# A second MLP product with five of its seven block products in matmuls of 512 columns and six rotating accumulator banks

## The chip, the cores and the metric

The kernel runs on one core of a Trainium2 chip. The metric is the device time of one execution in microseconds. A core has a matrix engine (PE, TensorE, whose weight loads are listed as PEld), a vector engine (DVE, VectorE), a scalar engine (ACT, ScalarE), GpSimd (POOL), and queues for DMA, here mostly SP's. Matmuls accumulate in PSUM, which has eight banks of 512 float32 columns on 128 partitions.

## The reference

```python
def _B_ref(x, w1, b1, w2, b2):
    h = _layernorm(x, axis=-1)                  # (B, S, D), S = 2048, D = 512
    u = jnp.einsum("bsd,sf->bdf", h, w1) + b1   # F = 1792
    u = _gelu(u)
    y = jnp.einsum("bdf,fs->bds", u, w2) + b2
    return y.transpose(0, 2, 1)

h = x + _A_ref(_layernorm(x), ...)   # linear attention with 32 heads and a learned feature map
out = h + _B_ref(_layernorm(h), w1, b1, w2, b2)
```

What changes is the product with `w2` ("the second product"): out of 1792 by 512 values of `u` and 1792 by 2048 weights it makes 2048 by 512 sums, to which `b2` and `h` are added.

## The kernel before

The attention block comes first, then the first MLP product (with `w1`, lines 62 to 64, matmuls of 512 columns), then GELU, then the second product, which is the last stage.

All products are of float32 accuracy on a faster matmul type: each operand is split into a high part, rounded to that type, and a low part, the rest. A product is the sum of high x high, high x low and low x high, so three matmuls.

The second product cuts the 2048 output rows into 16 tiles of 128 rows and takes them in 8 pairs (`sp`). The 1792 rows of `w2` are 14 tiles, taken in 7 pairs (`p`), so that there are 56 steps (`STEPS`), pair by pair. A step multiplies a 2 by 2 block matrix of weights (blocks of 128 x 128) with a 2 by 2 block matrix of `u` (blocks of 128 x 256, `HD` = 256 being half of the 512 columns). Instead of eight block products it makes seven, by the Strassen-Winograd scheme: seven weight operands (four of them sums of blocks) and seven operands of `u` (prepared once, `UB`), and a few additions at the end of each pair.

Weights are streamed in groups of two steps (`GRP` = 2, `stream_w2`): two loads of 256 KB on SP's queue into `wraw` (three buffers), four sums on DVE (lines 777 to 780, for both steps at once, 256 elements each), then the high part `whi` on ACT (line 57, 1792 elements) and the low part `wlo` on DVE (line 58). `whi` and `wlo` have two buffers each, so a group's buffers are filled again once PE has read the group two before.

Each product of a step is three matmuls of 256 columns (`product`, line 789) into one half of one of four banks; partial sums that belong to the same output accumulate in the same half, over all 7 steps of the pair. The pairs use two sets of four banks in turn (`ps_b`, or `ps_f` and `ps_q`). In a pair's last step the products are taken by bank, and then a copy on ACT (line 820) and five DVE operations (821 to 825) combine the banks, with `b2` added, into `ot`, and two DMAs on POOL's queue add `ot` to `out`, where `h` was stored before. The last pair instead adds to copies of its two output tiles (`hb`, lines 830 to 847), takes its last two steps together by bank, and stores the result.

The order of instructions on each engine in this stage is not the program's: the framework plans it when the kernel is built, in order of the times it expects, so PE may take a product's matmuls later than the loops name them.

Of the kernel before, what the change touches and what calls it, by code (L numbers as in the profile page):

```python
# [9 lines left out]
F32 = mybir.dt.float32  # L10
F32R = mybir.dt.float32r
AF = mybir.ActivationFunctionType
ALU = mybir.AluOpType
# [4 lines left out]
P = 128  # L18
S, D, H, DH, F = 2048, 512, 32, 16, 1792
NT = S // P  # L20
KD = D // P
NF = F // P
NG = 8
NPR = 2 * NG
Q_AT = (4, 6, 8, 9, 11, 13)
# [8 lines left out]
def block_kernel(ctx: ExitStack, tc: tile.TileContext, x, xT, wT, phic, wo, w1, b1, w2, b2,  # L34
                 kvmask, ident_in, out):
    nc = tc.nc
# [7 lines left out]
    mhalf = cst.tile([P, 4], F32, name="mhalf")  # L44
    b1s = cst.tile([P, NF], F32, name="b1s")
    b2s = cst.tile([P, NT], F32, name="b2s")
# [21 lines left out]
    ps_q = ctx.enter_context(tc.tile_pool(name="ps_q", bufs=2, space=PSUM, side="right"))  # L68
# [19 lines left out]
    wvl = wp.tile([P, KD, D], F32R, name="wvl")  # L88
    zacc = wp.tile([P, NG, P], F32, name="zacc")
    ps_k = a1.enter_context(tc.tile_pool(name="ps_k", bufs=2, space=PSUM))  # L90
# [85 lines left out]
    def k_ops(t, o):  # L176
        PK[t] = kk.tile([P, NG, P], F32, name="pk", bufs=len(V_NOT) + 3)
        run(logit_ops(o, PK[t], False))
# [180 lines left out]
    q = {"mm": 0, "logits": 0, "exp": 0, "sum": 0}  # L359
# [6 lines left out]
    def q_logits(lag):  # L366
        n = q["logits"]
        if n < min(NT, q["mm"] - lag + NT * (q["mm"] == NT)):
            EQ[n] = big.tile([P, NG, P], F32, name="eq", tag="big")
            q["logits"] += 1  # L370
# [28 lines left out]
    for t in range(3, NT - 1):  # L399
        if t + 2 < NT:  # L400
            raw = load_x(t + 2)
# [38 lines left out]
    def s_ez(t):  # L440
        EZ[t] = az.tile([P, NG, P], F32, name="ez")
        nc.gpsimd.tensor_mul(EZ[t], EQ[t], zB)  # L442
# [69 lines left out]
    ps_f = ctx.enter_context(tc.tile_pool(name="ps_f", bufs=2, space=PSUM, reuse_waits="tile"))  # L512
# [79 lines left out]
        split(HN[t][:, 0], HN[t][:, 1], hn, nc.gpsimd)  # L592

    w1v = w1.rearrange("(k p) f -> p k f", p=P)
    w2v = w2.rearrange("(k p) s -> p k s", p=P)

    LATER = []

# [15 lines left out]
    PU, WI, LO = {}, {}, []  # L614
    FN, FL = [0] * (NF // 2), [0] * (NF // 2)

# [90 lines left out]

    NP = NF // 2  # L710
    HD = D // 2
    up = ctx.enter_context(tc.tile_pool(name="up", bufs=1, side="right", reuse_waits="tile"))
    uo = ctx.enter_context(tc.tile_pool(name="uo", bufs=2, side="right", reuse_waits="tile"))
    ws = ctx.enter_context(tc.tile_pool(name="ws", bufs=2, side="right", reuse_waits="tile"))
    ur = ctx.enter_context(tc.tile_pool(name="ur", bufs=4, side="right", reuse_waits="tile"))
    ut = ctx.enter_context(tc.tile_pool(name="ut", bufs=1, side="right", reuse_waits="tile"))
    ps_b = ctx.enter_context(tc.tile_pool(name="ps_b", bufs=4, space=PSUM, reuse_waits="tile"))
# [3 lines left out]
    U, UB, far = {}, {}, {}  # L721
# [39 lines left out]
    hp = ctx.enter_context(tc.tile_pool(name="hp", bufs=1, reuse_waits="tile"))  # L761

    STEPS = [(sp, p) for sp in range(NT // 2) for p in range(NP)]
    GRP = 2
    AW = {}

    def stream_w2(n):
        steps = STEPS[n:n + GRP]
        raw = ws.tile([P, GRP, 7, P], F32, name="wraw", bufs=3)
        wh_ = ws.tile([P, GRP, 7, P], F32R, name="whi")  # L770
        wl_ = ws.tile([P, GRP, 7, P], F32R, name="wlo")
        for i, (sp, p) in enumerate(steps):
            nc.sync.dma_start(raw[:, i, 0:4].rearrange("p (k i) s -> p k (i s)", k=2),
                              w2v[:, 2 * p:2 * p + 2, sp * 2 * P:(sp + 1) * 2 * P])
            AW[sp, p] = wh_[:, i], wl_[:, i]
        with tc.issue_after(LO[-18]):
            nc.vector.tensor_add(raw[:, :, 4], raw[:, :, 0], raw[:, :, 2])
            nc.vector.tensor_sub(raw[:, :, 0], raw[:, :, 1], raw[:, :, 0])
            nc.vector.tensor_sub(raw[:, :, 5], raw[:, :, 4], raw[:, :, 1])
            nc.vector.tensor_sub(raw[:, :, 6], raw[:, :, 3], raw[:, :, 5])  # L780
        split(wh_, wl_, raw, nc.vector)


    PROD = ((1, 1, 0, 0, True), (2, 6, 2, 1, True), (3, 3, 3, 1, True), (4, 4, 2, 0, False), (0, 0, 1, 0, True),
            (5, 5, 0, 1, False), (6, 2, 3, 0, False))

    def product(o, a, b, start, stop):
        for i, (x, y) in enumerate(((0, 0), (0, 1), (1, 0))):
            nc.tensor.matmul(o, a[x], b[:, y], start=start and i == 0, stop=stop and i == 2, skip_group_check=True)  # L789

    def products(sp, ps, order):
        for a, b, bk, half, opens in order:
            for p in ps:
                wh_, wl_ = AW[sp, p]
                product(bank[bk][:, half], (wh_[:, a], wl_[:, a]), UB[p, b], p == 0 and opens, p == NP - 1)

    def flat(a):
        return a.rearrange("p k d -> p (k d)")

    for n, (sp, p) in enumerate(STEPS):  # L800
        t = 2 * sp
        last = t + 2 == NT
        if n % GRP == 0:
            stream_w2(n)
        if p == 0:
            pools = [ps_f, ps_f, ps_q, ps_q] if sp % 2 else [ps_b] * 4
            bank = [pool.tile([P, 2, HD], F32, name="py", tag="pu") for pool in pools]
        if p < NP - 1 - last:
            products(sp, [p], PROD)
            continue  # L810
        if p < NP - 1:
            continue
        by_bank = sorted(PROD, key=lambda m: m[2:4])
        e = uo.tile([P, 2, HD], F32, name="e")
        u2 = uo.tile([P, HD], F32, name="u2", bufs=1)
        u3 = uo.tile([P, HD], F32, name="u3")
        if not last:
            products(sp, [p], by_bank)
            ot = uo.tile([P, 2, 2, HD], F32, name="ot", bufs=1)
            nc.scalar.activation(e[:, 1], bank[0][:, 0], AF.Copy)  # L820
            nc.vector.tensor_add(u2, bank[0][:, 1], e[:, 1])
            nc.vector.tensor_add(u3, bank[1][:, 0], u2)
            nc.vector.tensor_add(e[:, 0], bank[2][:, 0], u2)
            for i, add in enumerate((u3.unsqueeze(1).to_broadcast([P, 2, HD]), e)):
                nc.vector.scalar_tensor_tensor(ot[:, i], bank[2 + i], b2s[:, t + i:t + i + 1], add,  # L825
                                               op0=ALU.add, op1=ALU.add)
                nc.gpsimd.dma_start(out[(t + i) * P:(t + i + 1) * P, :], flat(ot[:, i]), accum_op=ALU.add)  # L827
            continue

        hb = [hp.tile([P, 2, HD], F32, name=f"hb{i}") for i in range(2)]  # L830
        for i in range(2):
            nc.sync.dma_start(flat(hb[i]), out[(t + i) * P:(t + i + 1) * P, :])
            nc.vector.tensor_scalar(hb[i], hb[i], b2s[:, t + i:t + i + 1], None, op0=ALU.add)
        products(sp, [p - 1, p], by_bank)
        nc.scalar.activation(e[:, 1], bank[0][:, 0], AF.Copy)
        nc.vector.tensor_add(hb[1][:, 1], bank[0][:, 0], hb[1][:, 1])
        nc.vector.tensor_add(u2, bank[0][:, 1], e[:, 1])
        nc.vector.tensor_add(hb[1][:, 0], u2, hb[1][:, 0])
        nc.vector.tensor_add(u3, bank[1][:, 0], u2)
        nc.vector.tensor_add(hb[0], hb[0], u3.unsqueeze(1).to_broadcast([P, 2, HD]))  # L840
        nc.vector.tensor_add(hb[0][:, 0], bank[2][:, 0], hb[0][:, 0])
        nc.vector.tensor_add(hb[1][:, 0], bank[2][:, 0], hb[1][:, 0])
        nc.vector.tensor_add(hb[0][:, 1], bank[2][:, 1], hb[0][:, 1])
        nc.sync.dma_start(out[t * P:(t + 1) * P, :], flat(hb[0]))
        for k, q in ((0, nc.scalar), (1, nc.sync)):
            nc.vector.tensor_add(hb[1][:, k], bank[3][:, k], hb[1][:, k])
            q.dma_start(out[(t + 1) * P:NT * P, k * HD:(k + 1) * HD], hb[1][:, k])


def _layout(A_x, A_wqkv, A_w_phi, A_wo, B_w1, B_b1, B_w2, B_b2):  # L850
    x = np.asarray(A_x)[0]
    wqkv = np.asarray(A_wqkv)
    phi = np.asarray(A_w_phi)

    phic = np.concatenate([phi.reshape(4, P, DH).transpose(1, 0, 2).reshape(P, 64),
                           np.kron(np.eye(8), np.ones((DH, 1)))], axis=1).astype(np.float32)
    mask = np.zeros((P, 64), np.float32)
    for a in range(P // DH):
        for c in range(2):
            f = (2 * c + a % 2) * DH  # L860
            mask[a * DH:(a + 1) * DH, f:f + DH] = 1.0

    wo = np.asarray(A_wo).reshape(2, 4, 2, 32, D).transpose(2, 0, 1, 3, 4).reshape(D, D)
    return {
        "x": x,
        "xT": x.reshape(NT, P, KD, P).transpose(0, 3, 2, 1),
        "wT": wqkv.T,
        "phic": phic,
        "wo": wo,
        "w1": np.asarray(B_w1),  # L870
        "b1": np.asarray(B_b1).reshape(NF, P).T,
        "w2": np.asarray(B_w2),
        "b2": np.asarray(B_b2).reshape(NT, P).T,
        "kvmask": mask,
        "ident": np.eye(P, dtype=np.float32),
    }
# [18 lines left out]
```

## Time and profile before

| | |
|---|---|
| time, median of 3 runs | 534.46 us (534.25 to 535.26) |
| span of the profiled execution, first to last instruction | 532.6 us |
| its own whole time | not recorded apart from the span; the median run is 1.8 us above the span |
| mean granted TensorE clock | 0.998 |
| second product's matmuls | from 385.8 us to the last start at 526.8 us |
| matmuls in all | 3616 |

Times in the profile are in microseconds from the span's start. A row of the timeline has start, duration, engine, line, operation, output and inputs, shapes and the count of instructions merged into it; in brackets stands the time for which the engine was idle before it and what ended that. Matmuls are pipelined, so consecutive ones overlap in the records, and their cost is the distance from start to start. The rows that matter are in the prediction.

### The profile page before, as it was taken

How to read it: one execution, taken by the hardware profiler on the slowest of the kernel's cores; microseconds unless marked ns; L12 is line 12 of the kernel's file. 1: busy time of each engine (PE TensorE's matmuls, PEld its weight loads, DVE VectorE, ACT ScalarE, POOL GpSimd, SP SyncE). 2: the span in 40 equal slices, each digit the busy share in tenths (PEclk: the TensorE clock that was granted, in tenths of full speed). 3: DMA queues.
4: the chain of work that ended last, by engine and by line, in shares of the span. 5: the costliest groups of instructions: out<-in, count | busy, mean ns of one | idle time of the engine just before them, and what ended most of it. 6: DMA issues, size and time to landing. Idle time of an engine off the chain costs nothing.

```text
span 532.6 us, 9386 instructions
## 1 busy us (share of the span) xinstructions
PE 520.8 (98%) x3616; PEld 448.7 (84%) x3616; DVE 384.4 (72%) x680; ACT 271.9 (51%) x460; POOL 234.8 (44%) x190
## 2 busy tenths in 40 slices
PE   8999999999999989999999999999999999999995
PEld 7888888886877767777788888888899999999995
DVE  6993999877699989875325524835668877887784
ACT  6998844424336776557746423525444243343340
POOL 2589699877889988887325000000001101100110
PEclk9999999999999999999999999999999999999999
DMA  8633310020502233334255333542014556535631
GB/s 309 206 110 118 99 22 21 1 72 9 160 0 79 82 101 116 104 116 136 85 176 159 98 100 98 159 117 82 20 41 107 143 148 153 123 120 136 143 75 46
DMA packets 45486, 55.81 MB, mean 105 GB/s; under 512 B 3969, under 2 KB 33025, under 8 KB 45441
## 3 DMA queue, kind: packets, MB, share of 16 engines
q1 hardware_dynamic: 43136, 51.38, 30.7%
q0 software_dynamic: 2016, 3.67, 5.5%
q8 instruction: 28, 0.46, 0.4%
q10 hardware_dynamic: 288, 0.17, 0.1%
q14 instruction: 18, 0.14, 0.1%
HBM read 46.81 MB, written 8.39 MB: 104 GB/s over the span
## 4 chain that ended last, share of the span: by engine, by line
PE 83%; POOL 9%; DVE 3%; ACT 2%; issue 1%; DVEq 0%; POOLq 0%; ACTq 0%
PE py L789 26%; PE pu L62 11%; PE pu L63 11%; PE pu L64 11%; POOL ez L442 4%; POOL eq L460 3%; PE pv L63 2%; PE pv L64 2%; PE pv L62 2%; PE pk_ps L62 2%; PE pk_ps L63 2%; PE pk_ps L64 2%; POOL hs L58 2%; PE po L62 1%; PE kvp L207 1%; PE po L63 1%
## 5 line engine op out<-in xcount | busy, mean ns | idle before, releaser
L827 POOL DMA_DIRECT2D out<-ot x14 | 12.5, 1001 | 212.2 <-DVE ot L825 212.2
L789 PE MATMUL py<-uf,whi 128*128 128x256 f32 x560 | 96.2, 283 | 0.0
L63 PE MATMUL pu<-hs,whi 128*128 128x512 f32 x224 | 87.6, 391 | 1.8 <-POOL hs L58 1.8
L602 DVE TENSOR_TENSOR wlo<-wraw,whi 128x512 fp32r<-128x512 f32 x56 | 50.3, 903 | 51.8 <-ACT whi L610 50.7
L57 ACT ACTIVATE whi<-wraw 128x1792 fp32r<-128x1792 f32 x28 | 47.7, 1705 | 77.9 <-PE py L789 73.8
L62 PE MATMUL pu<-hs,whi 128*128 128x512 f32 x224 | 87.4, 395 | 0.0
L64 PE MATMUL pu<-hs,wlo 128*128 128x512 f32 x224 | 87.2, 390 | 0.0
L789 PEld LDWEIGHTS py<-uf,whi 128*128 128x128 f32 x560 | 83.3, 192 | 0.0
L789 PE MATMUL py<-uf,wlo 128*128 128x256 f32 x280 | 69.9, 283 | 0.0
L58 DVE TENSOR_TENSOR wlo<-wraw,whi 128x1792 fp32r<-128x1792 f32 x28 | 56.6, 2022 | 15.4 <-ACT whi L57 15.4
L610 ACT ACTIVATE whi<-wraw 128x512 fp32r<-128x512 f32 x56 | 35.0, 627 | 47.0 <-PE pu L63 44.8
L63 PEld LDWEIGHTS pu<-hs,whi 128*128 128x128 f32 x224 | 42.1, 188 | 11.0 <-POOL hs L58 2.8
L62 PEld LDWEIGHTS pu<-hs,whi 128*128 128x128 f32 x224 | 42.0, 188 | 10.9 <-issue 2.5
L64 PEld LDWEIGHTS pu<-hs,wlo 128*128 128x128 f32 x224 | 42.0, 188 | 9.1 <-DVE wlo L602 0.4
L789 PEld LDWEIGHTS py<-uf,wlo 128*128 128x128 f32 x280 | 49.7, 192 | 0.0
L442 POOL TENSOR_TENSOR ez<-eq,zB 128x1024 f32<-128x1024 f32 x16 | 40.9, 2559 | 2.5 <-ACT zB L488 2.5
L789 PE MATMUL py<-un,whi 128*128 128x256 f32 x224 | 38.4, 283 | 0.0
L195 POOL TENSOR_TENSOR pk<-pk,sk 128x1024 f32<-128x1024 f32 x16 | 31.0, 1941 | 9.8 <-DVE sk L194 9.0
L460 POOL TENSOR_TENSOR eq<-eq,w 128x1024 f32<-128x1024 f32 x16 | 32.0, 1997 | 4.0 <-DVE w L457 4.0
L789 PEld LDWEIGHTS py<-un,whi 128*128 128x128 f32 x224 | 33.2, 192 | 0.1
L199 POOL TENSOR_TENSOR zacc<-zacc,pk 128x1024 f32<-128x1024 f32 x13 | 31.3, 2405 | 0.6
L58 POOL TENSOR_TENSOR hs<-hn,hs 128x512 fp32r<-128x512 f32 x16 | 21.4, 1340 | 17.5 <-ACT hs L57 15.6
(165 smaller groups left out, 1176.5 us busy)
## 6 DMA issues: line engine op xcount, KB each, us to landing
wraw<-in_w SPq DMA_DIRECT2D x112, 256.0 KB, 2.9
xraw<-in_xT SPq DMA_DIRECT2D x16, 256.0 KB, 3.1
xh<-in_x SPq DMA_DIRECT2D x16, 256.0 KB, 2.6
h<-in_x SPq DMA_DIRECT2D x16, 256.0 KB, 2.7
out<-h SPq DMA_DIRECT2D x16, 256.0 KB, 3.0
out<-ot POOLq DMA_DIRECT2D x14, 256.0 KB, 4.8
wraw<-in_wT SPq DMA_DIRECT2D x12, 256.0 KB, 5.0
wo<-in_wo SPq DMA_DIRECT2D x4, 256.0 KB, 3.6
```

Source lines behind the costliest of these rows:

```text
L57: nc.scalar.activation(hi, src, AF.Copy)
L58: lo_engine.tensor_sub(lo, src, hi)
L62: nc.tensor.matmul(o, ah, bh, start=first, stop=False)
L63: nc.tensor.matmul(o, ah, bl, start=False, stop=False)
L64: nc.tensor.matmul(o, al, bh, start=False, stop=last)
L195: nc.gpsimd.tensor_mul(heads(PK[t]), heads(PK[t]), sk.unsqueeze(2).to_broadcast([P, 2 * H, DH]))
L199: nc.gpsimd.tensor_add(zacc, zacc, PK[t])
L442: nc.gpsimd.tensor_mul(EZ[t], EQ[t], zB)
L460: nc.gpsimd.tensor_mul(heads(EQ[t]), heads(EQ[t]), W[t].rearrange("p g c h -> p (g c h)").unsqueeze(2).to_broadcast([P, 2 * H, DH]))
L602: LO.append(nc.vector.tensor_sub(wl_, raw, wh_).ins)
L610: nc.scalar.activation(wh_, raw, AF.Copy)
L789: nc.tensor.matmul(o, a[x], b[:, y], start=start and i == 0, stop=stop and i == 2, skip_group_check=True)
```

## The change

- Each pair takes six banks from a ring of all eight. Five of the seven products write both halves of a bank: one matmul of 512 columns multiplies the high weight with the high and the low part of `u` side by side (the two parts land in the two halves), and one of 256 columns adds the low weight times the high part to the first half. The other two products share one bank, a half each, and stay as they were. In the last pair the final product stays narrow too.
- The scheme's signs change, so that all four weight sums are additions on DVE.
- The last two steps of every pair, not only of the last, are taken together, product by product.
- The outputs of a pair are made by a copy on ACT and twelve DVE operations of 256 columns, since the halves of five banks must be added up.
- `w2` is laid out in groups, so that a group is one load of 512 KB, contiguous for each partition; the sums of both steps lie side by side.

```diff
-        raw = ws.tile([P, GRP, 7, P], F32, name="wraw", bufs=3)
...
-        for i, (sp, p) in enumerate(steps):
-            nc.sync.dma_start(raw[:, i, 0:4].rearrange("p (k i) s -> p k (i s)", k=2),
-                              w2v[:, 2 * p:2 * p + 2, sp * 2 * P:(sp + 1) * 2 * P])
+        raw = ws.tile([P, 7, GRP * P], F32, name="wraw", bufs=3)
...
+        nc.sync.dma_start(raw[:, 0:4], w2[g])
...
-            nc.vector.tensor_add(raw[:, :, 4], raw[:, :, 0], raw[:, :, 2])
-            nc.vector.tensor_sub(raw[:, :, 0], raw[:, :, 1], raw[:, :, 0])
-            nc.vector.tensor_sub(raw[:, :, 5], raw[:, :, 4], raw[:, :, 1])
-            nc.vector.tensor_sub(raw[:, :, 6], raw[:, :, 3], raw[:, :, 5])
+            nc.vector.tensor_add(raw[:, 4], raw[:, 0], raw[:, 2])
+            nc.vector.tensor_add(raw[:, 0], raw[:, 0], raw[:, 1])
+            nc.vector.tensor_add(raw[:, 5], raw[:, 4], raw[:, 1])
+            nc.vector.tensor_add(raw[:, 6], raw[:, 3], raw[:, 5])
...
-    PROD = ((1, 1, 0, 0, True), (2, 6, 2, 1, True), (3, 3, 3, 1, True), (4, 4, 2, 0, False), (0, 0, 1, 0, True),
-            (5, 5, 0, 1, False), (6, 2, 3, 0, False))
+    PROD = ((1, 1, 0, None), (5, 5, 1, None), (0, 0, 2, 0), (4, 4, 2, 1), (2, 6, 3, None), (6, 2, 4, None),
+            (3, 3, 5, None))
+    LAST = PROD[:-1] + ((3, 3, 5, 0),)
...
+    def product(o, half, a, b, first, start, stop):
+        if half is None:
+            nc.tensor.matmul(o, a[0], b, start=start, stop=stop, skip_group_check=True)
+            nc.tensor.matmul(o[:, 0], a[1], b[:, 0], start=False, stop=stop, skip_group_check=True)
+            return
...
-            pools = [ps_f, ps_f, ps_q, ps_q] if sp % 2 else [ps_b] * 4
-            bank = [pool.tile([P, 2, HD], F32, name="py", tag="pu") for pool in pools]
+            bank = []
+            for _ in range(6):
+                pool = (ps_f, ps_q, ps_b, ps_b)[n_bank % 8 // 2]
+                bank.append(pool.tile([P, 2, HD], F32, name="py", tag="pu"))
+                n_bank += 1
...
+        products(sp, [p - 1, p], order)
...
             nc.scalar.activation(e[:, 1], bank[0][:, 0], AF.Copy)
-            nc.vector.tensor_add(u2, bank[0][:, 1], e[:, 1])
-            nc.vector.tensor_add(u3, bank[1][:, 0], u2)
-            nc.vector.tensor_add(e[:, 0], bank[2][:, 0], u2)
...
+            nc.vector.tensor_add(e[:, 1], bank[0][:, 1], e[:, 1])
+            nc.vector.tensor_sub(u2, bank[1][:, 0], e[:, 1])
+            nc.vector.tensor_add(u2, bank[1][:, 1], u2)
+            nc.vector.tensor_sub(u3, u2, bank[2][:, 0])
+            nc.vector.scalar_tensor_tensor(e[:, 0], bank[2][:, 1], -1.0, u2, op0=ALU.mult, op1=ALU.subtract)
...
+            def out_block(i, h, o, add, low=None):
+                nc.vector.scalar_tensor_tensor(ot[:, i, h], o, b2s[:, t + i:t + i + 1], add, op0=ALU.add, op1=ALU.add)
+                if low is not None:
+                    nc.vector.tensor_add(ot[:, i, h], low, ot[:, i, h])
...
+            out_block(0, 0, bank[2][:, 1], u3)
+            out_block(0, 1, bank[3][:, 0], u3, bank[3][:, 1])
...
+            out_block(1, 0, bank[4][:, 0], e[:, 0], bank[4][:, 1])
+            out_block(1, 1, bank[5][:, 0], e[:, 1], bank[5][:, 1])
```

More of the change, by code (lines that the diff above doesn't have):

```diff
@@ L22 @@
 NF = F // P
+NP = NF // 2
+HD = D // 2
+GRP = 2
 NG = 8
@@ L594, in block_kernel @@
     w1v = w1.rearrange("(k p) f -> p k f", p=P)
-    w2v = w2.rearrange("(k p) s -> p k s", p=P)
     LATER = []
@@ L699, in block_kernel @@
     aq.close()
-    NP = NF // 2
-    HD = D // 2
     up = ctx.enter_context(tc.tile_pool(name="up", bufs=1, side="right", reuse_waits="tile"))
@@ L763, in block_kernel @@
     STEPS = [(sp, p) for sp in range(NT // 2) for p in range(NP)]
-    GRP = 2
     AW = {}
     def stream_w2(n):
-        steps = STEPS[n:n + GRP]
-        raw = ws.tile([P, GRP, 7, P], F32, name="wraw", bufs=3)
-        wh_ = ws.tile([P, GRP, 7, P], F32R, name="whi")
-        wl_ = ws.tile([P, GRP, 7, P], F32R, name="wlo")
-        for i, (sp, p) in enumerate(steps):
-            nc.sync.dma_start(raw[:, i, 0:4].rearrange("p (k i) s -> p k (i s)", k=2),
-                              w2v[:, 2 * p:2 * p + 2, sp * 2 * P:(sp + 1) * 2 * P])
-            AW[sp, p] = wh_[:, i], wl_[:, i]
+        g = n // GRP
@@ L776, in stream_w2 @@
+        raw = ws.tile([P, 7, GRP * P], F32, name="wraw", bufs=3)
+        wh_ = ws.tile([P, 7, GRP * P], F32R, name="whi")
+        wl_ = ws.tile([P, 7, GRP * P], F32R, name="wlo")
+        nc.sync.dma_start(raw[:, 0:4], w2[g])
+        for i, step in enumerate(STEPS[n:n + GRP]):
+            AW[step] = wh_[:, :, i * P:(i + 1) * P], wl_[:, :, i * P:(i + 1) * P]
         with tc.issue_after(LO[-18]):
-            nc.vector.tensor_add(raw[:, :, 4], raw[:, :, 0], raw[:, :, 2])
-            nc.vector.tensor_sub(raw[:, :, 0], raw[:, :, 1], raw[:, :, 0])
@@ L787, in product @@
-    def product(o, a, b, start, stop):
+    PROD = ((1, 1, 0, None), (5, 5, 1, None), (0, 0, 2, 0), (4, 4, 2, 1), (2, 6, 3, None), (6, 2, 4, None),
[6 more added lines that the diff above has]
+            return
@@ L788, in product @@
         for i, (x, y) in enumerate(((0, 0), (0, 1), (1, 0))):
-            nc.tensor.matmul(o, a[x], b[:, y], start=start and i == 0, stop=stop and i == 2, skip_group_check=True)
+            nc.tensor.matmul(o[:, half], a[x], b[:, y], start=start and first and i == 0, stop=stop and i == 2,
+                             skip_group_check=True)
     def products(sp, ps, order):
-        for a, b, bk, half, opens in order:
+        for a, b, bk, half in order:
             for p in ps:
                 wh_, wl_ = AW[sp, p]
-                product(bank[bk][:, half], (wh_[:, a], wl_[:, a]), UB[p, b], p == 0 and opens, p == NP - 1)
+                product(bank[bk], half, (wh_[:, a], wl_[:, a]), UB[p, b], half != 1, p == 0, p == NP - 1)
@@ L797, in flat @@
     def flat(a):
         return a.rearrange("p k d -> p (k d)")
+    n_bank = 0
     for n, (sp, p) in enumerate(STEPS):
@@ L805, in block_kernel @@
         if p == 0:
-            pools = [ps_f, ps_f, ps_q, ps_q] if sp % 2 else [ps_b] * 4
-            bank = [pool.tile([P, 2, HD], F32, name="py", tag="pu") for pool in pools]
-        if p < NP - 1 - last:
-            products(sp, [p], PROD)
+            bank = []
[3 more added lines that the diff above has]
+                n_bank += 1
+        order = LAST if last else PROD
+        if p < NP - 2:
+            products(sp, [p], order)
             continue
@@ L812, in block_kernel @@
             continue
-        by_bank = sorted(PROD, key=lambda m: m[2:4])
+        products(sp, [p - 1, p], order)
         e = uo.tile([P, 2, HD], F32, name="e")
@@ L817, in block_kernel @@
         if not last:
-            products(sp, [p], by_bank)
             ot = uo.tile([P, 2, 2, HD], F32, name="ot", bufs=1)
             nc.scalar.activation(e[:, 1], bank[0][:, 0], AF.Copy)
-            nc.vector.tensor_add(u2, bank[0][:, 1], e[:, 1])
-            nc.vector.tensor_add(u3, bank[1][:, 0], u2)
-            nc.vector.tensor_add(e[:, 0], bank[2][:, 0], u2)
[L824 to L827, printed above, removed]
+            nc.vector.tensor_add(e[:, 1], bank[0][:, 1], e[:, 1])
[9 more added lines that the diff above has]
+            out_block(0, 1, bank[3][:, 0], u3, bank[3][:, 1])
+            nc.gpsimd.dma_start(out[t * P:(t + 1) * P, :], flat(ot[:, 0]), accum_op=ALU.add)
+            out_block(1, 0, bank[4][:, 0], e[:, 0], bank[4][:, 1])
+            out_block(1, 1, bank[5][:, 0], e[:, 1], bank[5][:, 1])
+            nc.gpsimd.dma_start(out[(t + 1) * P:(t + 2) * P, :], flat(ot[:, 1]), accum_op=ALU.add)
             continue
@@ L833, in block_kernel @@
             nc.vector.tensor_scalar(hb[i], hb[i], b2s[:, t + i:t + i + 1], None, op0=ALU.add)
-        products(sp, [p - 1, p], by_bank)
         nc.scalar.activation(e[:, 1], bank[0][:, 0], AF.Copy)
[L836 to L839, printed above, removed]
+        nc.vector.tensor_add(e[:, 1], bank[0][:, 1], e[:, 1])
+        nc.vector.tensor_add(hb[1][:, 1], e[:, 1], hb[1][:, 1])
+        nc.vector.tensor_sub(u2, bank[1][:, 0], e[:, 1])
+        nc.vector.tensor_add(u2, bank[1][:, 1], u2)
+        nc.vector.tensor_sub(hb[1][:, 0], hb[1][:, 0], u2)
+        nc.vector.tensor_sub(u3, u2, bank[2][:, 0])
+        nc.vector.tensor_sub(hb[1][:, 0], hb[1][:, 0], bank[2][:, 1])
         nc.vector.tensor_add(hb[0], hb[0], u3.unsqueeze(1).to_broadcast([P, 2, HD]))
-        nc.vector.tensor_add(hb[0][:, 0], bank[2][:, 0], hb[0][:, 0])
-        nc.vector.tensor_add(hb[1][:, 0], bank[2][:, 0], hb[1][:, 0])
-        nc.vector.tensor_add(hb[0][:, 1], bank[2][:, 1], hb[0][:, 1])
+        nc.vector.tensor_add(hb[0][:, 0], bank[2][:, 1], hb[0][:, 0])
+        nc.vector.tensor_add(hb[0][:, 1], bank[3][:, 0], hb[0][:, 1])
+        nc.vector.tensor_add(hb[0][:, 1], bank[3][:, 1], hb[0][:, 1])
         nc.sync.dma_start(out[t * P:(t + 1) * P, :], flat(hb[0]))
-        for k, q in ((0, nc.scalar), (1, nc.sync)):
-            nc.vector.tensor_add(hb[1][:, k], bank[3][:, k], hb[1][:, k])
-            q.dma_start(out[(t + 1) * P:NT * P, k * HD:(k + 1) * HD], hb[1][:, k])
+        nc.vector.tensor_add(hb[1][:, 0], bank[4][:, 0], hb[1][:, 0])
+        nc.vector.tensor_add(hb[1][:, 0], bank[4][:, 1], hb[1][:, 0])
+        nc.scalar.dma_start(out[(t + 1) * P:NT * P, 0:HD], hb[1][:, 0])
+        nc.vector.tensor_add(hb[1][:, 1], bank[5][:, 0], hb[1][:, 1])
+        nc.sync.dma_start(out[(t + 1) * P:NT * P, HD:D], hb[1][:, 1])
 def _layout(A_x, A_wqkv, A_w_phi, A_wo, B_w1, B_b1, B_w2, B_b2):
@@ L861, in _layout @@
             mask[a * DH:(a + 1) * DH, f:f + DH] = 1.0
+    w2 = np.asarray(B_w2).reshape(NP, 2, P, NT // 2, 2, P).transpose(3, 0, 2, 1, 4, 5)
+    w2 = w2.reshape(-1, GRP, P, 4, P).transpose(0, 2, 3, 1, 4).reshape(-1, P, 4, GRP * P)
     wo = np.asarray(A_wo).reshape(2, 4, 2, 32, D).transpose(2, 0, 1, 3, 4).reshape(D, D)
@@ L871, in _layout @@
         "b1": np.asarray(B_b1).reshape(NF, P).T,
-        "w2": np.asarray(B_w2),
+        "w2": w2,
         "b2": np.asarray(B_b2).reshape(NT, P).T,
```

## The prediction

> **What bounds the kernel now.** I read the page first (busy shares, clock, chain), then the instructions of line 789, then the waits and the timeline of the second product.
>
> ```profile
> span 532.6 us, 9386 instructions
> PE 520.8 (98%) x3616; PEld 448.7 (84%) x3616; DVE 384.4 (72%) x680; ACT 271.9 (51%) x460; POOL 234.8 (44%) x190
> PEclk9999999999999999999999999999999999999999
> PE 83%; POOL 9%; DVE 3%; ACT 2%; issue 1%; DVEq 0%; POOLq 0%; ACTq 0%
> ...
> L789 PE MATMUL py<-uf,whi x560: 283/283/283, 390.9 to 526.7; 128*128 128x256 f32 x187
> L789 PE MATMUL py<-uf,wlo x280: 279/283/283, 391.1 to 526.8; 128*128 128x256 f32 x140
> L789 PE MATMUL py<-un,whi x224: 278/283/283, 385.8 to 514.1; 128*128 128x256 f32 x112
> L789 PE MATMUL py<-un,wlo x112: 283/283/283, 386.1 to 514.2; 128*128 128x256 f32 x112
> ```
>
> PE carries 83% of the chain at full clock. The second product is 560 + 280 + 224 + 112 = 1176 matmuls of 256 columns that start from 385.8 to 526.8 us: 141.0 / 1175 = 0.120 us from start to start. A duration of 283 ns is no cost here: matmuls overlap, and the pitch is what PE pays. The stage is PE's as long as the others keep up, and the waits say how closely they do:
>
> ```profile
> ACT whi L57 <- PE py L789: 73.8, 25, 3.3
> DVE wlo L58 <- ACT whi L57: 14.9, 12, 3.0
> DVE wraw L777 <- DMA wraw<-in_w: 11.5, 7, 3.3
> ...
> 391.00:523.00 132.00, 132.00 (x1103) 132.00 (x1102) 102.17 (x153) 46.98 (x33) 12.48 (x14) 1.00 0.50 120
> ```
>
> The first three are waits of the stage (total us, times, longest), the last a stretch: PE, PEld, DVE, ACT and POOL busy, clock, DMA share, GB/s. ACT waits for PE to give a weight buffer back: the ring of two groups goes PE, ACT (high part), DVE (low part), PE. No row has PE waiting. DVE works 102.2 of 132 us, so about 30 us are free.
>
> **PE's saving.** Five of seven products become one matmul of 512 columns (high weight on high and low operand together) and one of 256, in place of three of 256. The price of 512 columns stands in the first MLP product, just before:
>
> ```profile
> 383.11 0.39 PE L62 MATMUL pu<-hs,whi 128*128 128x512 f32 x1
> ...
> 385.15 0.39 PE L62 MATMUL pu<-hs,whi 128*128 128x512 f32 x1
> ```
>
> Nine matmuls lie between (one each of lines 62, 63, 64, three times): 2.04 / 9 = 0.2267 us. Two narrow ones cost 0.2400, so a merge saves 0.0133. Merged are 7 pairs x 7 steps x 5, and 7 x 4 in the last pair, whose final product stays narrow: 273 merges, 3.6 us. Both shapes have the same fixed part if columns cost the same: 0.2267 - 0.1200 = 0.1067 for 256 columns, so 0.0133 lies on each instruction, and that is what goes. The bounds are 0 (two narrow ones are no cheaper merged in this mixture) and 3.6; I take 3.6, since line 62's rows are the same shape, each with its own weight load. A step is then 5 x 0.3467 + 2 x 0.360 = 2.45 us instead of 2.52, a pair 17.2 instead of 17.6. The Trainium skill, "TensorE: Matmul & The Clock Gate", section "Back-to-back issue gap", speaks against the size of this: it gives columns at 2.4 GHz plus about 2.5 ns each, so that 273 merges would be worth an estimated 0.7 us. By that rule, the trace agrees on the slope, but its fixed part is 13.3 ns, and the measured pitch decides.
>
> **DVE's new work.** The high and low halves of a product now lie in separate halves of a bank and must be added on DVE. Prices, alone and interleaved:
>
> ```profile
> 433.05 2.03 DVE L58 TENSOR_TENSOR wlo<-wraw,whi 128x1792 fp32r<-128x1792 f32 x1
> 434.99 0.42 DVE L777 TENSOR_TENSOR wraw<-wraw 128x256 f32<-128x256 f32 x1
> 435.44 0.43 DVE L778 TENSOR_TENSOR wraw<-wraw 128x256 f32<-128x256 f32 x1
> 435.79 0.42 DVE L779 TENSOR_TENSOR wraw<-wraw 128x256 f32<-128x256 f32 x1
> 436.24 0.42 DVE L780 TENSOR_TENSOR wraw<-wraw 128x256 f32<-128x256 f32 x1
> 438.09 2.03 DVE L58 TENSOR_TENSOR wlo<-wraw,whi 128x1792 fp32r<-128x1792 f32 x1 [1.43 <-ACT whi L57]
> 440.03 0.42 DVE L777 TENSOR_TENSOR wraw<-wraw 128x256 f32<-128x256 f32 x1
> 440.37 0.42 DVE L821 TENSOR_TENSOR u<-py,e 128x256 f32<-128x256 f32 x1
> 440.70 0.41 DVE L778 TENSOR_TENSOR wraw<-wraw 128x256 f32<-128x256 f32 x1
> ...
> 442.37 0.74 DVE L825 SCALAR_TENSOR_TENSOR ot<-py,b2s,u 128x512 f32<-128x512 f32 x1
> 443.03 0.74 DVE L825 SCALAR_TENSOR_TENSOR ot<-py,b2s,e 128x512 f32<-128x512 f32 x1
> 443.69 2.01 DVE L58 TENSOR_TENSOR wlo<-wraw,whi 128x1792 fp32r<-128x1792 f32 x1
> ```
>
> By start to start: an operation of 256 costs 0.34 among independent ones (440.03, 440.37, 440.70) and 0.45 where the next needs its result (434.99 to 435.44); line 58 costs 1.94; line 825 on 512 columns 0.66. A line-825 operation of 256 is not in the trace; between 0.34 and 0.66 I take 0.39, which puts it as far above a plain 256 as 0.742 is above the 0.69 of a plain 512 (line 840, below). Before, a pair's outputs cost DVE 3 x 0.34 + 2 x 0.66 = 2.3 us. After, they are 7 plain and 5 line-825 operations of 256: 4.3 interleaved, and 5.0 if six stand behind the result they need. Added: 2.0 to 2.7 us per pair, 14 to 19 for seven pairs. The 102 us become 116 to 121, in about 128.5 us: 90 to 94% busy. So DVE's total still fits, and on average this work is hidden by PE's; what decides is when it falls.
>
> The sums of weights stay four DVE operations of 256 per group, with the same dependencies; additions instead of subtractions cost nothing, hidden as now. The two 256 KB loads per group become one of 512 KB from a layout that is contiguous per partition: fewer pieces, nothing moved past on SP. Its landing lies ahead of the sums, and DVE's 11.5 us of waiting for such loads is cover; a later landing costs nothing until it exceeds the idle 30 us less the 19 added.
>
> **Where it falls.** Six of eight rotating banks leave two free: a pair's banks 2 to 5 are banks 0 to 3 of the pair before. And the last two steps are now run together, product by product. In 4 of the 8 pairs (0, 2, 4, 6) these steps lie in two weight groups, so the older group comes back at the pair's end, not one step before. The ring's times:
>
> ```profile
> 436.35 1.71 ACT L57 ACTIVATE whi<-wraw 128x1792 fp32r<-128x1792 f32 x1 [3.33 <-PE py L789]
> 438.34 0.38 ACT L820 ACTIVATE e<-py 128x256 f32<-128x256 f32 x1 [0.28 <-PE py L789]
> 441.39 1.71 ACT L57 ACTIVATE whi<-wraw 128x1792 fp32r<-128x1792 f32 x1 [2.67 <-PE py L789]
> ...
> 400.94 1.12 PE L789 MATMUL py<-uf,whi 128*128 128x256 f32 x8
> 401.90 0.64 PE L789 MATMUL py<-un,whi 128*128 128x256 f32 x4
> 402.38 0.28 PE L789 MATMUL py<-uf,wlo 128*128 128x256 f32 x1
> ```
>
> High part at 436.35, low part at 438.09, done at 440.12: the ring takes 3.8 us. Against it works PE's order: it does not follow the loops, but runs high-weight matmuls first (8, one product in each of four banks, I infer) while a low part is late. After, six banks allow 5 x 0.227 + 2 x 0.120 = 1.4 us of such work. For pairs 0, 2, 4, 6, with the pair's end at zero: the high buffer is last read by a matmul that starts at -0.69 and takes 0.39; ACT starts at about -0.2 and ends at 1.5, line 58 runs from 1.5 to 3.6. The next pair's second step starts at 2.45, and with the high parts first needs the low part at 3.8. It just fits, if DVE is free at 1.5. The banks: bank 0 is ready at about -4.0, bank 3 at -1.1, DVE has nine operations on banks 0 to 3, some 3.6 us with its ACT copy ahead; the next pair needs old bank 0 at 0.7, old bank 3 at 2.1. That fits too, unless line 58 stands ahead of them. I take 0.3 us of waiting over the whole stage, near zero since both cases fit; the ends are 0 and 8.5 (the first rival).
>
> **The tail.** The last pair's own chain:
>
> ```profile
> 524.68 0.42 DVE L836 TENSOR_TENSOR hb<-py,hb 128x256 f32<-128x256 f32 x1 [3.92 <-ACT e L835]
> 525.02 0.41 DVE L837 TENSOR_TENSOR u<-py,e 128x256 f32<-128x256 f32 x1
> 525.47 0.42 DVE L838 TENSOR_TENSOR hb<-u,hb 128x256 f32<-128x256 f32 x1
> ...
> 526.26 0.69 DVE L840 TENSOR_TENSOR hb<-hb,u 128x512 f32<-128x512 f32 x1
> 527.06 0.42 DVE L841 TENSOR_TENSOR hb<-py,hb 128x256 f32<-128x256 f32 x1
> ...
> 528.06 0.75 DVE L846 TENSOR_TENSOR hb<-py,hb 128x256 f32<-128x256 f32 x2
> 528.84 0.36 SPq L847 DMA_DIRECT2D out<-hb  x1
> ```
>
> Ten operations take from 524.68 to 528.81, 4.1 us, and DVE hardly waits after the first. PE's last matmul starts at 526.8, so its stream ends near 526.94, and DVE ends 1.9 us later. After, 14 operations: 5 steps of 0.45, 7 of 0.34, one of 0.80 (line 840 to 841) and the last one's 0.42 make 5.9 us. They begin earlier: bank 0 takes 4 matmuls (0.69 us) of the last two steps instead of 12 (1.44), so 0.75 sooner than today's 2.8 us into them, at 2.0. These steps last 4.94 us, so DVE ends 2.0 + 5.9 - 4.9 = 3.0 us after PE. Tail: +1.1 us, with ends of 0.4 (the copy follows bank 0 at once) and 1.8 (no earlier start). The final stores are unchanged.
>
> **Sum.** -3.6 + 1.1 + 0.3 = -2.2 us. The profiled execution's span of 532.6 becomes 530.4; the median of the runs, 534.46, lies 1.8 above that span, and what lies around the span is untouched: 532.3 us.
>
> **The rivals.** *First, slower: DVE makes PE wait at the pairs' ends.* If the outputs stand ahead of line 58 on DVE, they end at about 2.8 (bank 5's after zero) and with the next sums among them at 3.4; line 58 then ends at 5.4, 1.6 us after PE needs it. Four such pairs cost 6.6 us. In the other pairs the low part goes first (-3.0 to -1.1), outputs and sums take until 4.9, the next line 58 until 6.9 against a need at 6.3: 0.6 us, three times. With 6.6 to 8.5 us of waits the sum is +4.1 to +6.0, about 539.5. It decides from 2.5 us, 0.36 per pair. For it: 90 to 94% load on a queue in order, and outputs stood ahead of line 58 at 442.37 to 443.69. Against: today that costs no gap on PE, and high-first order absorbs lateness. Chance 0.22.
>
> *Second, a merged matmul saves nothing.* The sum is 1.1 + 0.3: 535.9, slower. Against it stand line 62's rows. 0.06.
>
> *Third, part of the waits come:* 1.1 to 3.3 us of them eat the gain, time within 0.2% (1.07 us, about what a measurement here can tell from no change), near 534.4. 0.13.
>
> That the merging does not happen would show as 1176 matmuls; the loop issues 1176 - 273 = 903. 0.01.
>
> **How the numbers follow.** My forecast has 0.58: 532.3, its own range 530.8 (no waits and a tail of 0.4 make 531.3, and the three runs before spread by 1 us, of which I allow half) to 533.4. The range reaches to 538.0, about half of the first rival, leaving some 0.11 above and 0.06 below. Faster 0.58; same 0.13; slower 0.29.
>
> **What would show it.** Right: 512-column rows of the second product 0.227 us apart, 903 matmuls, no PE gap above 0.1 us in the stage, DVE 90 to 94% busy, DVE's last operation 2.3 to 3.7 us after PE's stream. Wrong: PE gaps at the pairs' ends released by DVE's low part (line 58) or by a bank's output addition, or a wide pitch near 0.24.

## The result and the profile after

The changed kernel takes 556.91 us (median of 4 runs, 556.89 to 557.54) against 534.43 us: a ratio of 1.0419, 95% interval 1.0404 to 1.0434. The forecast was 532.3, and the range ended at 538.0.

The page after (span; PE's row of section 1; PE's busy tenths in 40 slices; its clock; the chain by engine):

```profile
span 555.1 us, 8834 instructions
PE 526.7 (95%) x3343; PEld 434.0 (78%) x3343; DVE 399.7 (72%) x733; ACT 270.8 (49%) x460; POOL 234.5 (42%) x190
PE   8999999999999989999999999999989979979975
PEclk9999999999999999999999999999999999999999
PE 64%; DVE 13%; POOL 9%; DMA 5%; ACT 5%; issue 3%; DVEq 0%; ACTq 0%; POOLq 0%
```

PE's row of the page before:

```profile
PE   8999999999999989999999999999999999999995
```

Where it had only nines, in the last quarter, there are holes now; the clock is full. The chain went to PE for 83%, to DVE for 3% and to ACT for 2%; it goes to PE for 64%, DVE and ACT have grown, and DMA has come in. The wide matmuls are there, 195 + 78 = 273 (line 788, count, durations, first and last start):

```profile
L788 PE MATMUL py<-uf,whi x195: 387/396/505, 391.2 to 548.2; 128*128 128x512 f32 x195
L788 PE MATMUL py<-un,whi x78: 387/398/504, 386.3 to 535.6; 128*128 128x512 f32 x78
```

The second product starts at 386.26 us and its last matmul at 549.06, so it takes 162.8 us instead of 141.0: the 22.5 us of the span are 21.8 here, 0.4 of later start and 0.3 after the last matmul. The waits of PE's weight loads in that stage (total us, times, longest), which before had no row:

```profile
PEld py L789 <- DVE wlo L61: 12.6, 16, 1.3
PEld py L788 <- ACT whi L60: 9.8, 11, 1.3
PEld py L792 <- DVE e L829: 2.7, 3, 1.2
PEld py L788 <- issue: 1.2, 4, 0.3
```

Of 26.3 us, 22.4 wait for a low or a high weight part (lines 61 and 60, the lines 58 and 57 of before), only 2.7 for a bank (line 829 is an output's first addition). So PE runs out of weights, in two ways. The timeline shows the first:

```profile
412.38 3.29 ACT L60 ACTIVATE whi<-wraw 128x1792 fp32r<-128x1792 f32 x2 [7.28 <-PE py L788]
414.13 0.30 PEld L788 LDWEIGHTS py<-uf,whi 128*128 128x128 f32 x2 [1.34 <-ACT whi L60]
414.11 3.96 DVE L61 TENSOR_TENSOR wlo<-wraw,whi 128x1792 fp32r<-128x1792 f32 x2 [0.89 <-ACT whi L60]
416.19 0.30 PEld L789 LDWEIGHTS py<-uf,wlo 128*128 128x128 f32 x2 [0.84 <-DVE wlo L61]
420.87 0.43 DVE L775 TENSOR_TENSOR wraw<-wraw 128x256 f32<-128x256 f32 x1 [2.80 <-DMA wraw<-in_w]
```

ACT waits 7.3 us and then makes two high parts in a row; DVE follows with two low parts in a row, PE waits for each, and then DVE waits for the raw weights, whose buffers had come free together too. Before, ACT's high parts came one by one, 5.04 us apart. Two groups' buffers are being given back at once, and the ring of two starts from empty. Seven such refills make about 13.4 of the 22.4 us.

The other 9.0 us, in nine waits, come around the pairs' ends, where a high part is ready and DVE has not yet come to the low one:

```profile
403.39 1.70 ACT L60 ACTIVATE whi<-wraw 128x1792 fp32r<-128x1792 f32 x1
...
405.38 0.41 DVE L778 TENSOR_TENSOR wraw<-wraw 128x256 f32<-128x256 f32 x1
405.71 0.41 DVE L831 TENSOR_TENSOR u<-py,u 128x256 f32<-128x256 f32 x1
406.04 2.01 DVE L61 TENSOR_TENSOR wlo<-wraw,whi 128x1792 fp32r<-128x1792 f32 x1
...
408.11 0.30 PEld L789 LDWEIGHTS py<-un,wlo 128*128 128x128 f32 x2 [1.34 <-DVE wlo L61]
```

The high part ends at 405.09; weight sums and output operations stand ahead of the low part, which starts 0.9 us later. Ten low parts of the stage start 0.9 to 2.1 us behind their high parts.

Why two groups come back together stands in the order of PE's instructions in the built program, here from the first pair's end (the rows are numbered with equal neighbours merged; py_4276 to py_4279 are banks 2 to 5 of the second pair; whi_4214 is the group of the first pair's last and the second pair's first step, whi_4297 the group after it):

```
1644 L792 py_4276<-un0,whi_4214 [waits DVE]
1649 L788 py_4274<-un1,whi_4297 [waits Activation]
1652 L788 py_4277<-un0,whi_4214 [waits DVE,PE]
...
1671 L788 py_4278<-un0,whi_4214 [waits DVE]
1675 L788 py_4278<-uf_3990,whi_4297
1677 L788 py_4279<-un0,whi_4214 [waits DVE,PE]
1678 L789 py_4279<-un0,wlo_4215
1681 L788 py_4279<-uf_3990,whi_4297
1683 L788 py_4274<-uf_4010,whi_4339 [waits Activation]
```

The first step's products into banks that are not free yet are put off, behind products of the second and third step into banks that are. Group 4214, whose work could end with the first step, is last read in row 1678, when group 4297 has all but four of its matmuls behind it. Both come back at once.

### The profile page after: what moved, and what is told of

Its sections match the earlier page's. It is cut to its first block, busy times and chain, and to the rows that moved or that the text cites. A ratio compares the mean times of both kernels' runs of the same rounds, so it can differ in the third digit from the quotient of the medians.

```text
span 555.1 us, 8834 instructions
## 1 busy us (share of the span) xinstructions
PE 526.7 (95%) x3343; PEld 434.0 (78%) x3343; DVE 399.7 (72%) x733; ACT 270.8 (49%) x460; POOL 234.5 (42%) x190
## 4 chain that ended last, share of the span: by engine, by line
PE 64%; DVE 13%; POOL 9%; DMA 5%; ACT 5%; issue 3%; DVEq 0%; ACTq 0%; POOLq 0%
PE pu L65 11%; PE pu L66 10%; PE pu L67 10%; DVE wlo L61 6%; DMA wraw<-in_w 5%; PE py L788 4%; POOL ez L445 3%; PE py L792 3%; PE py L789 3%; POOL eq L463 2%; ACT whi L60 2%; PE pv L66 2%; PE pv L67 2%; PE pv L65 2%; PE pk_ps L65 2%
## 5 line engine op out<-in xcount | busy, mean ns | idle before, releaser
L842 POOL DMA_DIRECT2D out<-ot x7 | 6.2, 888 | 232.2 <-DVE ot L838 232.2
L788 PE MATMUL py<-uf,whi 128*128 128x512 f32 x195 | 67.4, 400 | 6.4 <-ACT whi L60 6.4
L789 PE MATMUL py<-uf,wlo 128*128 128x256 f32 x195 | 47.4, 285 | 2.4 <-DVE wlo L61 2.4
L788 PEld LDWEIGHTS py<-uf,whi 128*128 128x128 f32 x195 | 34.0, 188 | 12.4 <-ACT whi L60 8.5
L789 PEld LDWEIGHTS py<-uf,wlo 128*128 128x128 f32 x195 | 34.5, 189 | 6.4 <-DVE wlo L61 5.0
L792 PE MATMUL py<-uf,whi 128*128 128x256 f32 x170 | 32.9, 281 | 0.0
L792 PEld LDWEIGHTS py<-uf,whi 128*128 128x128 f32 x170 | 27.6, 189 | 2.5
L788 PE MATMUL py<-un,whi 128*128 128x512 f32 x78 | 28.6, 406 | 0.6 <-DVE u L831 0.2
```

Source lines behind the costliest of these rows:

```text
L788: nc.tensor.matmul(o, a[0], b, start=start, stop=stop, skip_group_check=True)
L789: nc.tensor.matmul(o[:, 0], a[1], b[:, 0], start=False, stop=stop, skip_group_check=True)
L792: nc.tensor.matmul(o[:, half], a[x], b[:, y], start=start and first and i == 0, stop=stop and i == 2, skip_group_check=True)
```

## The experiments

Three theories were put against each other: A, the products put off for a bank hold their weight group; B, the joined last two steps hold the older group; C, DVE has too much output work. A time without a median is one run; the kernel before took 534.4 to 535.2 us on the chips used, so a difference under 1 us between single runs says nothing. The first four runs:

**Three weight buffers** on the changed kernel:

```diff
+    wx = ctx.enter_context(tc.tile_pool(name="wx", bufs=1, reuse_waits="tile"))
...
-        wh_ = ws.tile([P, 7, GRP * P], F32R, name="whi")
+        wh_ = (wx if n // GRP % 3 == 2 else ws).tile([P, 7, GRP * P], F32R, name="whi")
```

and the same for `wlo`.

> The changed kernel with three buffers instead of two for the high and low weight parts; nothing else. Theory A (the products of a new pair whose banks are not free yet are put off, and hold their weight group so long that the ring of two runs dry): a third group breaks the hold, PE's waits in the second product fall from 25 us to under 8, 531 to 539 us. Theory B (taking the last two steps of every pair together holds the older group): also 531 to 539 us, since a third buffer covers that as well. Theory C (DVE has too much output work): no change, 550 to 557 us.

542.95 us, beside 535.23 of the kernel before on that chip: 14 us of the loss go, not all, and the time lies above what A and B had. C as it was put (no change) is out. But a longer ring also covers a low part that DVE makes late, so this run does not tell the hold from DVE's lateness.

**The last step alone** on the changed kernel:

```diff
-        products(sp, [p - 1, p], order)
+        products(sp, [p - 1, p] if last else [p], order)
```

and the step before the last taken by itself in all pairs but the last.

> The changed kernel, but only the last pair takes its last two steps together, as before the change. Theory A: the bank waits stay, 545 to 555 us. Theory B: most of the loss goes, 532 to 540 us. Theory C: 553 to 558 us.

562.33 us, slower than every theory had it. Its waits of weight loads:

```profile
PEld py L789 <- DVE wlo L61: 16.8, 16, 3.1
PEld py L788 <- ACT whi L60: 9.8, 10, 1.3
PEld py L788 <- DVE ot L836: 1.3, 1, 1.3
```

Joining helps this kernel. By the order of the products it completes banks 0 to 3 earlier before the pair's end, which I take for the reason; no run separates it. Most of the extra 5.4 us is clock: three waits of 2.5 to 2.7 us are each followed by 3.4 us at half clock, in which 39 narrow and 3 wide matmuls lie, an estimated 4.2 us by the pitches of the last section.

**The joined steps alone**, on the kernel before:

```diff
-            products(sp, [p], by_bank)
+            products(sp, [p - 1, p], by_bank)
```

with the step before the last left to it, as in the changed kernel.

> The kernel before, but every pair takes its last two steps together, by bank, as the changed kernel does; four banks a pair in two sets, narrow matmuls. Theory A: little, 534 to 539 us. Theory B: most of the loss appears, 545 to 556 us. Theory C: 534 to 536 us.

550.64 us against 535.23, with 12.4 us in waits for the low part:

```profile
PEld py L789 <- DVE wlo L58: 12.4, 5, 3.7
```

So B is a cause too, as large as it was forecast and far above what A had: on its own the joining costs 15 us with two buffers, some 2.5 of them by the clock. DVE has a part in it: where these waits fall, the low part stands behind the weight sums and the five output operations (448.20 against a high part that ended at 445.52).

**Less output work** on the changed kernel: the second `u2` addition and the three `low` additions are dropped.

> The changed kernel without four of the twelve DVE operations of each of the first seven pairs' outputs (the additions of the lower halves of banks 1, 3, 4 and 5 are left out). Theory A: banks come back about 1.5 us sooner, part of the loss goes, 545 to 552 us. Theory B: 553 to 557 us. Theory C: most goes, 532 to 540 us.

555.97 us. A third of DVE's output operations less buys 0.9 us at most; one stretch at half clock, an estimated 1.6 us, is in this time (last section). C, by which most of the loss would go, is out; A, too, had expected more here, and only B had this. What the run does not change is DVE's order: around the pairs' ends the low parts still start 1.3 to 3.1 us behind their high parts.

**Late banks alone**, on the kernel before:

```diff
-            pools = [ps_f, ps_f, ps_q, ps_q] if sp % 2 else [ps_b] * 4
+            pools = [(ps_b, ps_b, ps_f)[(4 * sp + i) % 6 // 2] for i in range(4)]
```

> The kernel before (narrow matmuls, four banks a pair, five DVE operations, last step alone), but the banks come from a ring of six instead of two sets of four, so that two of a pair's four banks are those of the pair before. Theory A (products put off for a bank hold their weight group): PE waits at the pairs' starts, 536 to 548 us, milder than in the changed kernel, since only two of seven products' banks, not four of six, have to come back. Theory B (the joined last two steps): 534 to 536 us. Theory C (DVE's output work): 534 to 536 us.

540.57 us, as A had it. Matmuls, DVE work and loads are those of before, and only two of four banks come back late; PE then waits, and again not for banks:

```profile
PEld py L789 <- DVE wlo L58: 4.3, 4, 1.1
PEld py L789 <- ACT whi L57: 2.1, 4, 0.6
```

Here the low parts of these waits start at most 0.5 us behind their high parts: it is the refill from empty alone, four times.

**Early banks** in the changed kernel:

```diff
+            for i in range(1, 4):
+                held = hp.tile([P, 2, HD], F32, name=f"held{i}")
+                nc.scalar.activation(held, bank[i], AF.Copy)
+                bank[i] = held
```

> The changed kernel, but ACT copies banks 1 to 3 of each of the first seven pairs to SBUF as soon as they are complete, and DVE works from the copies; DVE's operations stay as many. Theory A: these banks, which the next pair needs, come back without waiting for DVE's queue, the put-off products come earlier, 538 to 548 us. Theory B: 553 to 557 us, or worse by the copies' place on ACT. Theory C: 553 to 557 us.

544.89 us: 12 us of the loss go although ACT has more to do and DVE no less; two stretches at half clock, an estimated 3.1 us, are still in it. What stays of waits is the low part (9.2 us):

```profile
PEld py L789 <- DVE wlo L61: 9.2, 6, 2.4
PEld py L788 <- ACT whi L60: 0.5, 2, 0.2
```

**Three buffers and the last step alone** (both edits above):

> The changed kernel with three weight buffers and with the last step of a pair alone. Of theory A, with joining as a help to the banks (which the run without joining showed): 545 to 552 us, worse than 543 with three buffers and joined steps. If instead joining costs once the ring is long enough: 535 to 541 us.

548.22 us against 542.95 with joined steps, as A had it: while banks are late, joining helps. One stretch at half clock makes an estimated 1.5 of the 5.3 us.

**Early banks and the last step alone**, two buffers:

> ACT copies of banks 1 to 3, two weight buffers, last step of a pair alone. If the joined steps are what is left of the loss with copies (544.9): 534 to 541 us. If early banks need the joined steps: 546 to 560 us.

538.42 us against 544.89 with joined steps. Once banks are early, joining costs 6.5 us with two buffers, about half of it by the clock: the joined version has two stretches at half clock, this one none.

**Both cures**, early banks and three buffers, steps joined as in the change:

> The changed kernel with both cures: ACT copies of banks 1 to 3, and three weight buffers; last two steps joined. Theory A with the joined steps as a second holder of the ring: of 25 us of PE waits under 6 stay, 531.5 to 538 us; none at all would be 136.9 + what lies around, about 531. If the two cures only cover the same loss: 540 to 545 us.

531.62 us (median of 4) against 534.81: 0.9941, interval 0.9925 to 0.9958. No wait of PE's stays in the stage, and this version beats both kernels.

**Both cures, the last step alone:**

> Both cures, and the last step of a pair alone, as before the change. If joining is a holder of the ring once banks come back early: like or better than the joined one, 531 to 536 us. If joining still helps the banks: 537 to 548 us.

533.88 us, 0.9978 (0.9967 to 0.9989): better than before, less than with joined steps; one gap of 1 us is left in its trace. So joining is no loss with three buffers.

**The two holders alone, with a third weight buffer**, on the kernel before:

> The kernel before with the ring of six banks, and three weight buffers. If late banks cost time only by holding weight groups: back to 533 to 536 us from 540.6. If PE waits for the banks themselves: 538 to 541 us.

> The kernel before with the last two steps of every pair joined, and three weight buffers. If joining costs by holding the older weight group: back to 533 to 537 us from 550.6. If it costs otherwise: 545 to 551 us.

534.71 and 534.24 us, beside 535.16: back from 540.57 and 550.64. With one more slot in the ring neither holder costs anything that a single run can tell, though in the joined one low parts still start up to 2.4 us behind their high parts.

**One merged product on the kernel before:** `(0, 0)`, which has bank 1 to itself, as a matmul of 512 columns and one of 256, and one more addition into `u3`.

> The kernel before with one of its seven products merged into a matmul of 512 columns: the one that has a bank to itself, so that four banks a pair in two sets suffice; one more DVE addition per pair. 55 or 56 merges of 13.3 ns are 0.74 us. If only the banks were the trouble and DVE has room: 533.5 to 534.0 against 534.4. If an added DVE operation alone upsets the ring: 535 us or more.

534.66 us, 0.9998 (0.9989 to 1.0007). The time is as before: neither the forecast of a gain nor that of a loss came true. The stage is 0.8 us shorter in the trace (140.2), as forecast for 56 merges, and 0.5 us of it is given back after the last matmul, where DVE, with the addition more, ends 0.5 us later.

**The layout of the weights alone**, on the kernel before:

> The kernel before with the new layout of the weights alone (one load of 512 KB per group, sums of both steps side by side); signs, banks and matmuls as before. All theories: no cost, 534 to 535 us; a clear loss here would mean that the load or the planner's new order, not the banks, has a share.

533.93 us, 0.9986 (0.9976 to 0.9995): no loss; a gain of 0.7 us that no theory had. The stage is as long as before (140.99 us); the stretch after the last matmul is 0.75 shorter. From DVE's last result to the span's end it takes 3.1 us in every run with the new layout and 3.8 in every run with the old; why was not sought.

## Why the prediction was wrong

**The step that failed is "Where it falls".** It put the banks and the weight ring to the test one by one, each against the loops' own times, and took 0.3 us of waits; the trace has 22.4 us for weights and 2.7 for banks. The check of the ring followed the older of the joined steps' groups alone, and let the next pair's second step start 2.45 us after the pair's end, that is, the first one end there and give its group back. But a bank that is late moves that step's products behind two later steps, and the group with them. The prediction had even quoted the planner's habit of taking other matmuls first, as a cover (1.4 us of high-weight work); that the same habit holds buffers was not seen.

The same step let the low part (line 61, then 58) follow its high part at once, "if DVE is free". DVE was not: sums and outputs stood first, as in the rows from 403.39 on.

**The first rival was right in part.** It put DVE's outputs ahead of the low part, at 6.6 to 8.5 us, and the nine waits of that kind come to 9.0. The refills from empty, 13.4 us, it did not have. Nor does that order cost anything where the ring has room: in the version with both cures ten low parts start 0.8 to 1.6 us behind their high parts (one high part ends at 422.57, its low part starts at 424.11), and PE never waits. Line 61 put ahead of the outputs was not run; how much that alone would cure stays open.

**The joined steps** were seen as a hold and sized as one that "just fits". Alone they cost 15 us with two buffers and nothing with three. In the changed kernel, with two buffers, they are both: a cost of 6.5 us if banks are early, a help of 5 if they are late, the clock included. One cannot add such terms up.

**PE's saving** was over-sized. Without any gap, in the version with both cures, the pitch is to be read directly (lines 789 and 790 there are the wide and the narrow one):

```profile
460.09 0.40 PE L789 MATMUL py<-un,whi 128*128 128x512 f32 x1
460.32 0.28 PE L790 MATMUL py<-un,wlo 128*128 128x256 f32 x1
460.44 0.40 PE L789 MATMUL py<-uf,whi 128*128 128x512 f32 x1
460.67 0.28 PE L790 MATMUL py<-uf,wlo 128*128 128x256 f32 x1
460.79 0.40 PE L789 MATMUL py<-uf,whi 128*128 128x512 f32 x1
```

A product takes 0.35 us (460.09 to 460.79 for two); over the stage a wide one followed by a narrow one has a mean pitch of 0.236 and the narrow one behind it 0.117, 0.353 together, against the 0.3467 assumed and 0.360 for three narrow ones. The stage runs from 386.00 to 524.90, 138.9 us, so 2.1 us are saved, not 3.6. The lesser 0.7 us, estimated from the Trainium skill's fixed part of 2.5 ns per matmul ("TensorE: Matmul & The Clock Gate", "Back-to-back issue gap"; the section gives it for an isolated gap), is too small; the truth lies between. The saving of a merge is not one number: 273 merges save 2.1 us here, 8 ns each, while the 56 of the kernel with one merged product saved 0.8, 14 ns each. Why is not shown.

**DVE's load was about right.** Busy time of PE, PEld, DVE, ACT and POOL, of the changed kernel and of the version with both cures:

```profile
391.00:545.00 154.00, 137.61 (x845) 117.64 (x844) 116.31 (x204) 46.16 (x33) 12.36 (x14) 1.00 0.43 103
...
391.00:520.00 129.00, 129.00 (x838) 117.22 (x838) 114.02 (x208) 56.51 (x53) 12.35 (x14) 1.00 0.49 123
```

In these stretches DVE works 116 and 114 us, at the lower end of the forecast (116 to 121) or just below, and is 88% busy where PE never waits, against 90 to 94. It fits, as the prediction said; the sum was just not what decides.

**The tail's sum held, its terms less so.** The last pair's chain in the changed kernel:

```profile
546.58 0.42 DVE L853 TENSOR_TENSOR e<-py,e 128x256 f32<-128x256 f32 x1 [4.14 <-ACT e L852]
...
551.64 0.41 DVE L863 TENSOR_TENSOR hb<-py,hb 128x256 f32<-128x256 f32 x1
...
549.06 0.28 PE L792 MATMUL py<-uf,wlo 128*128 128x256 f32 x1
```

DVE ends at 552.05, 2.9 us after PE's stream (549.06 + 0.12), where 3.0 were forecast and 1.9 stood before. Two errors cancel in it: the chain takes 5.5 us, not 5.9, and starts 2.6 us before the stream's end, not 2.9. And the span ends only 0.3 us later after the last matmul, not 1.1: the stretch from DVE's last result to the span's end shrank from 3.8 to 3.1 us, as it did with the new layout alone. In the version with both cures the chain starts 3.7 us before the stream's end, and DVE ends 1.95 us after it, hardly later than before.

That version's 531.62 us lies near the forecast of 532.3, but by luck. Against the span before, its terms are -2.1 us (PE), +0.1 (tail), -0.75 (the stretch after DVE's last result) and +0.2 (later start), where the prediction had -3.6 (PE), +1.1 (tail) and +0.3 (waits).

## What to carry to other kernels

A planner or a queue that takes other work while one input is late keeps every other buffer of the postponed work occupied: with two rings (accumulator banks and streamed weights) a shortage in one shows up as a wait in the other, and the profile names the second. Before taking slack out of one ring, look at what a late slot of it holds elsewhere, and try one more slot of that: here 14 KB per partition of weight buffers and an early copy out of three banks turned a loss of 4.2% into a gain of 0.6%. Two buffers given back at once (two refills in a row behind a long idle time) are the sign to look for.

## What the runs showed of the hardware

A long wait can cost more than itself. In the kernel before with joined steps, PE waits 3.5 us for one low part, and then runs at half its clock for 5.7 us (three stretches follow the timeline's rows; the number behind the five engines' busy times is the clock):

```profile
450.27 1.01 PE L789 MATMUL py<-un,wlo 128*128 128x256 f32 x3 [3.48 <-DVE wlo L58]
451.08 0.63 PE L789 MATMUL py<-un,whi 128*128 128x256 f32 x2
451.51 0.63 PE L789 MATMUL py<-un,wlo 128*128 128x256 f32 x2
...
440.00:446.00 6.00, 6.00 (x52) 5.99 (x51) 2.73 (x9) 2.35 (x3) 0.00 (x0) 1.00 0.28 90
450.30:456.00 5.70, 5.70 (x27) 5.70 (x28) 1.91 (x2) 0.00 (x0) 0.00 (x0) 0.50 1.03 230
456.00:462.00 6.00, 6.00 (x52) 6.00 (x52) 5.00 (x9) 1.70 (x1) 0.00 (x0) 1.00 0.12 40
```

Matmuls of 256 columns are then about 0.213 us apart instead of 0.120 (451.08 to 451.51 is two), which cost this run an estimated 2.5 us of its 15 (27 matmuls). The changed kernel with the last step alone shows the same three times, after waits of 2.5 to 2.7 us. The changed kernel itself, where PE stood still for 1.0 us at most, kept its clock.

The length of one wait does not decide, though. The joined kernel before kept its clock at a wait of 2.8 us (before 528.89), and of five waits of 1.7 to 1.8 us in the kernel with less output work only the last was followed by a lower clock, 0.52 from 531.5 to 534.8. By the traces' records of the clock, each such stretch of the stage lasts 3.41 us, once twice that, and those of one run begin on a grid of 3.41 us. In the eight windows of that grid that end in a drop, PE's busy time by the profile is 0.94 to 1.66 us; of the other windows at full clock, in all runs, one has 1.66 and the rest 1.74 or more. So in this stage it was a window less than about half busy that cost the clock, and the wait of 2.8 us, which the grid splits (1.85 and 2.20 us busy), cost none. The Trainium skill, "TensorE: Matmul & The Clock Gate", "The HAM clock gate", has the array fall to half its clock after an idle window of about 3.4 us, with the window running freely, and return after a busy one. The traces agree on the half clock, the window's length and its free running; but a window did not have to be idle here: 1.66 us of work in 3.41 were once too few.
